# Query sums on VectorE, scaling on GpSimd ahead of the turn, and shared tokens' loads without overlap, in the opening of an attention and Fourier-mix kernel

## The chip, the cores and the metric

The kernel runs on one core of a Trainium2 chip. The metric is device time in microseconds (us), as a median of runs. In the profile PE is TensorE (matrix products; PEld its weight loads), DVE is VectorE, ACT is ScalarE, POOL is GpSimd, and SP is SyncE, which here issues most DMA loads. L12 is line 12 of the kernel. Each engine works through its own queue in order and waits for other engines by semaphores.

## The reference

```python
# q, k, v: (8, 8, 576, 64); w_ch1: (512, 2048); w_ch2: (2048, 512); all float32
def _attn_ref(q, k, v):
    q_s = np.exp(q - np.max(q, axis=-1, keepdims=True))
    q_s = q_s / (np.sum(q_s, axis=-1, keepdims=True) + 1e-09)
    k_s = np.exp(k - np.max(k, axis=2, keepdims=True))
    k_s = k_s / (np.sum(k_s, axis=2, keepdims=True) + 1e-09)
    kv = np.einsum('bhsd,bhse->bhde', k_s, v)
    return np.einsum('bhsd,bhde->bhse', q_s, kv).astype(np.float32)

def _moe_ref(x, w_ch1, w_ch2):          # x: attention output as (8, 576, 512)
    X = np.fft.fft(np.fft.fft(x, axis=1), axis=2)
    u = x + np.real(X).astype(np.float32)
    mu = np.mean(u, axis=-1, keepdims=True)
    var = np.mean((u - mu) ** 2, axis=-1, keepdims=True)
    un = (u - mu) / np.sqrt(var + 1e-06)
    return (u + np.maximum(un @ w_ch1, 0.0) @ w_ch2).astype(np.float32)
```

## The kernel before, in words

The eight sequences are worked on in turn. Each has 576 tokens: four tiles of 128 tokens (named by c and u, each 0 or 1), and 64 that are put together with those of a second sequence in a "shared" tile. Only the first 55 us differ between the two kernels: the opening, in which nothing of an earlier sequence is there to be overlapped with. After it TensorE does the two feed-forward products (L1169 and L1160 are the first of them, L1181 the second) of one sequence after another, and attention, Fourier mixing and norm of the next sequence run beside them.

The opening has its steps written out by hand: the string OPENING lists each step with a planned time, the steps are sorted by that time, and so every engine's queue gets its order. The planned time sets an order and nothing else. WARM adds groups of matrix products (L241) that have no use but to keep TensorE busy; they write the PSUM bank `ba`.

The steps, with the lines at which their instructions show:
- `k00` to `k03`: the first sequence's keys, two heads each. `max` (DVE L529), `exp` (ACT L532), `turn` (PE transposes L537), `four` (ACT copy of four transposed blocks, L540), `last` and `fifth` (transposes L545 and copy L548 of the last 64 tokens of all four), `kv` (PE L559). `k0 inverse` (DVE L551, L552) makes the reciprocal of the key sums, and `k0 scale0/1` (DVE L563) write the scaled product into `kvr`. `k10` to `k13` are the second sequence's keys.
- `A`, `B`, `C`, `D`: the first sequence's query tiles (c, u) = (0,0), (1,1), (0,1), (1,0); `t`: the shared tile. `max` (DVE L805), `less` (subtract the maximum: POOL L810, for `t` DVE), `exp` (ACT L814), `turn` (PE L822), `copy` (ACT L832, for `t` L842), `kv` (the product with `kvr`, PE L884, for `t` L914).
- The sums of the exponentials of A to D come from TensorE: `ones` (L876) multiplies the turned tile by a matrix of ones, `inverse` (DVE L890, L891) makes the reciprocals, and `out` (DVE L899) multiplies the product by them while it copies it from PSUM to the tile `x`. For `t` DVE does sum, reciprocal and multiplication ahead of the turn (L783 to L794).
- `t fold`, `t join` (DVE and POOL, L854 to L863) and `t parts`, `t folds` (ACT L921, L922; DVE L926 to L929) fold the shared tile for the Fourier transform. `tokens`, `columns`, `by`, `again` (DVE L945, L951, L958, L964 and L965) fold the four tiles; folds 0 and 2 read A and C, folds 1 and 3 read D and B.
- `b0` to `b4`: blocks of the first Fourier product (PE L997, L1000; copies on ACT L1007 to L1012). `m0`, `m1`: the second one for c = 0 and 1 (PE L1025; ACT L1034; DVE L1042; `add0` on DVE and `add1` on POOL, L1054 and L1055).
- `s00` and so on (statistics, DVE L1075), `root`, `scales`, `normal` (DVE L1096 for u = 0, ACT L1099 for u = 1), `turn` (PE L1105) and `laid` (DVE or ACT, L1114) end in the tile `unT`, which L1169 reads: first the columns of the tiles with c = 0, then those with c = 1.
- `c0`: the first of 32 "words" of the weights, which arrive as 64-bit values and are converted: `hi` and `lo` (ACT L375, L376), `shift` and `sign` (DVE L369, L372), `add` (POOL L377). Word i is needed by the i-th step of the first feed-forward product.

The loads are issued at the start (`loads_first`): keys, queries A/B, values, queries C/D, values, tables, the second sequence's keys and values and then the words on SP's queue, the shared tile's rows on ScalarE's.

Of the kernel before, what the change touches and what calls it, by code (L numbers as in the profile page):

```python
# [40 lines left out]
F32 = mybir.dt.float32  # L41
# [43 lines left out]
WARM = (3, 3), (24.7, 6), (41.9, 2), (43.45, 1), (44.5, 1)  # L85
OPENING = """
4.30 k00 max, 5.10 k00 exp, 5.50 k01 max, 6.05 k00 turn, 6.30 k01 exp, 6.65 k02 max, 7.06 k00 four,
7.25 k01 turn, 7.56 k02 exp, 7.75 k03 max, 8.32 k01 four, 8.51 k02 turn, 8.82 k03 exp, 8.90 A max, 9.50 B max,
9.58 k02 four, 9.65 A less, 9.77 k0 last, 10.10 k0 inverse, 10.27 k03 turn, 10.42 k0 fifth, 10.69 B less,
10.80 A exp, 11.20 k00 kv, 11.30 k03 four, 11.84 B exp, 11.85 A turn, 12.20 C max, 12.30 k01 kv, 12.45 A copy,  # L90
12.80 D max, 12.95 B turn, 12.95 C less, 13.40 A ones, 13.55 B copy, 13.99 D less, 14.10 C exp, 14.20 k02 kv,
14.35 A inverse, 14.85 C turn, 15.00 t max, 15.14 D exp, 15.30 k03 kv, 15.75 t less, 15.95 D turn,
16.35 k0 scale0, 16.40 B ones, 16.47 t exp, 16.80 k0 scale1, 17.14 t inverse, 17.25 B kv, 17.99 B inverse,
18.22 A kv, 18.35 C copy, 18.39 t normal, 19.01 B out, 19.19 t turn, 19.32 D copy, 19.63 k10 max, 19.69 C ones,
19.84 t copy, 20.30 A out, 20.43 k10 exp, 20.49 C kv, 20.92 C inverse, 21.39 t fold, 21.46 D ones,
22.09 t join, 22.26 D kv, 22.51 D inverse, 22.91 C out, 23.31 t kv, 23.53 D out, 24.15 tokens0, 24.21 k10 turn,
24.36 t parts, 24.77 tokens1, 25.39 columns0, 25.46 k10 four, 25.75 columns1, 26.23 by1, 26.59 by0,
26.80 c0 hi, 26.95 t folds, 27.45 c0 lo, 27.70 again0, 28.00 again1, 28.50 tokens3, 28.60 b0 times,
29.12 tokens2, 29.58 b1 times, 29.74 columns3, 29.80 b0 copies, 30.10 columns2, 30.56 b4 times, 30.58 by2,
30.78 b1 copies, 30.94 by3, 31.42 again2, 31.72 again3, 31.76 b4 copies, 32.22 k12 max, 32.32 b2 times,  # L100
32.89 c0 shift, 33.02 k12 exp, 33.30 b3 times, 33.59 c0 sign, 33.78 b2 copies, 34.19 k13 max, 34.28 k12 turn,
34.31 c0 add, 34.50 b3 copies, 34.86 k11 max, 35.05 k13 exp, 35.20 m0 times, 35.81 k12 four, 36.10 k13 turn,
36.31 m0 copy, 36.55 m1 times, 36.66 k11 exp, 36.81 m0 sums, 37.42 k13 four, 37.61 k1 last, 37.71 m0 add0,
37.92 m1 copy, 38.07 k11 turn, 38.27 k1 fifth, 38.39 m0 add1, 38.42 m1 sums, 38.77 k11 four, 38.92 k10 kv,
39.22 s00, 39.27 roots, 39.67 k11 kv, 39.69 m1 add1, 39.97 s01, 40.42 k12 kv, 40.87 root0, 40.99 m1 add0,
41.17 k13 kv, 41.67 scales0, 41.87 s11, 42.02 normal01, 42.62 s10, 42.77 turn01, 43.37 normal00, 43.52 root1,
43.87 scales1, 43.89 normal11, 43.95 laid01, 44.02 turn00, 44.22 normal10, 44.77 laid00, 44.87 turn10,
45.47 turn11, 45.62 laid10, 46.22 laid11, 53.00 k1 inverse, 53.30 k1 scale0, 53.60 k1 scale1"""
# [28 lines left out]
class _Block:  # L137
    def __init__(self, ctx, tc, q, kT, v, w1, w2, ft, cd, out):
# [38 lines left out]
        self.ones = c.tile([P, NR, H], F32, name="ones")  # L177
        nc.gpsimd.memset(self.ones[:], 0.0)
        for h in range(2):
            nc.gpsimd.memset(self.ones[64 * h:64 * h + 64].rearrange("p r h -> p (r h)")[:, h::H + 2], 1.0)  # L180

# [31 lines left out]
        self.unused = None  # L213
# [32 lines left out]
    def loads_first(self, fetch):  # L246
# [45 lines left out]
        def second(r):  # L292
# [7 lines left out]
                 lambda: values(0), lambda: queries(1), lambda: values(2), shared_firsts, self.tables,  # L300
# [214 lines left out]
    def first_keys(self, b):  # L515
# [4 lines left out]
        copy, box, top = nc.vector.tensor_copy if b == 0 else nc.scalar.copy, {}, {}  # L520
# [26 lines left out]
        def fifth():  # L547
            copy(self.fifth[64:], box["last"][64:])  # L548
# [26 lines left out]
    def opening(self, fetch, converted):  # L575
# [17 lines left out]
        named("t max,t less,t exp", self.q_exp_spread(shared, V))  # L593
        named("t inverse,t normal", self.q_inverse(shared, V, V))
# [203 lines left out]
    def q_exp_spread(self, it, e=None):  # L798
# [9 lines left out]
        def less():  # L808
            m = live[it].pop()[:].unsqueeze(2).to_broadcast([P, H, DH])
            (e or nc.gpsimd).tensor_tensor(out=heads(), in0=heads(), in1=m, op=ALU.add)  # L810
# [873 lines left out]
```

## Time and profile before

| | before |
|---|---|
| median of 3 runs | 1071.49 us (1070.27 to 1072.46) |
| the profiled execution | 1070.28 us |
| its span in the profile | 1068.5 us |
| PE busy / DVE busy / ACT busy / POOL busy | 1057.8 / 699.5 / 404.1 / 376.6 us |
| L1169, first half of the first feed-forward step, starts at | 49.08 us |
| L1160, its second step, starts at | 52.90 us |

A row of the timeline gives the start, the busy time, the engine, the line, the operation, the tiles (written <- read), how many instructions were merged into the row (x8), and in brackets how long the engine had been idle and what released it. One float32 product shows as two records.

### The profile page before, as it was taken

To read this page: it belongs to the slowest core of one execution; us is meant where nothing else is said; L and a number is where in the kernel's file an instruction comes from. 1 tells how busy PE (TensorE), PEld (TensorE's weight loads), DVE (VectorE), ACT (ScalarE), POOL (GpSimd) and SP (SyncE) were. 2 spreads that over 40 slices of the span, in tenths; PEclk is the share of its full clock that TensorE was granted. 3 is DMA by queue.
4 is the path that set the end of the run, shared out by engine and by line. 5 is a ranking of instruction groups with operands and counts; after the bars stand their busy time and mean duration, and the time that the engine had idled before them with its cause. 6 is when DMAs were issued, how large, how long until landed. Compare 5 with 4: busy or idle time off the path is not lost.

```text
span 1068.5 us, 16976 instructions
## 1 busy us (share of the span) xinstructions
PE 1057.8 (99%) x6394; PEld 922.1 (86%) x6394; DVE 699.5 (65%) x1350; ACT 404.1 (38%) x953; POOL 376.6 (35%) x317
## 2 busy tenths in 40 slices
PE   8999999999999999999999999999999999999998
PEld 7744556988898899889998999889988998899898
DVE  6897787685455884677555765678457754674563
ACT  5675534632245215531443234521552132231210
POOL 3262220265412733454515542374336450000000
PEclk9999999999999999999999999999999999999999
DMA  9496478648975576645755576557644575576464
GB/s 332 171 304 244 174 247 293 212 156 285 334 263 203 181 256 234 226 177 198 268 186 193 197 247 212 192 202 256 224 167 158 198 255 179 192 261 216 179 214 152
DMA packets 113546, 236.04 MB, mean 221 GB/s; under 512 B 23272, under 2 KB 74856, under 8 KB 102840
## 3 DMA queue, kind: packets, MB, share of 16 engines
q1 hardware_dynamic: 112904, 234.16, 63.9%
q8 instruction: 51, 0.84, 0.3%
q10 hardware_dynamic: 480, 0.52, 0.2%
q14 instruction: 31, 0.25, 0.1%
q0 software_dynamic: 80, 0.26, 0.1%
HBM read 199.79 MB, written 39.06 MB: 224 GB/s over the span
## 4 chain that ended last, share of the span: by engine, by line
PE 86%; DVE 3%; ACT 2%; issue 0%; ACTq 0%; DVEq 0%
PE bb L1244 15%; PE bb L1371 10%; PE bc L1244 10%; PE ba L1244 10%; PE bc L1371 7%; PE ba L1371 7%; PE bb L1341 5%; PE acc L716 3%; PE acc L884 2%; PE bc L1181 2%; PE bb L1460 2%; PE acc L997 2%; PE acc L1000 2%; PE acc L1025 2%; PE bc L1460 1%; PE ba L1460 1%
## 5 line engine op out<-in xcount | busy, mean ns | idle before, releaser
L1244 PE MATMUL bb<-unT,big 128*128 128x256 f32 x768 | 184.4, 380 | 0.8 <-DVE u L1214 0.8
L1244 PEld LDWEIGHTS bb<-unT,big 128*128 128x128 f32 x768 | 142.5, 190 | 20.3 <-DVE u L1214 2.3
L1256 ACT ACTIVATE big<-big 128x512 f32<-128x512 f32 x96 | 60.5, 630 | 195.0 <-DVE big L1255 194.5
L1244 PE MATMUL ba<-unT,big 128*128 128x256 f32 x512 | 123.8, 379 | 0.0
L1244 PE MATMUL bc<-unT,big 128*128 128x256 f32 x512 | 123.4, 379 | 0.0
L1214 DVE TENSOR_TENSOR u<-bb,s 128x512 f32<-128x512 f32 x66 | 45.6, 690 | 105.9 <-PE bb L1244 83.2
L383 POOL TENSOR_TENSOR big<-big 128x512 f32<-128x512 f32 x24 | 30.5, 1270 | 226.5 <-ACT big L1256 226.5
L1244 PEld LDWEIGHTS bc<-unT,big 128*128 128x128 f32 x512 | 94.7, 190 | 12.5 <-DVE big L1255 0.9
L1371 PE MATMUL bb<-big 128*128 128x128 f32 x848 | 105.1, 275 | 0.3 <-DVE u L1378 0.3
L1244 PEld LDWEIGHTS ba<-unT,big 128*128 128x128 f32 x512 | 94.4, 190 | 12.2 <-issue 0.5
L1371 PEld LDWEIGHTS bb<-big 128*128 128x128 f32 x848 | 99.6, 192 | 0.5 <-DVE u L1378 0.4
L1321 POOL TENSOR_TENSOR x<-x,big 128x512 f32<-128x512 f32 x45 | 57.7, 1297 | 62.7 <-issue 32.9
L1371 PE MATMUL ba<-big 128*128 128x128 f32 x640 | 79.6, 275 | 0.0
L766 ACT ACTIVATE q<-q,qm 128x64 f32<-128x64 f32 x248 | 67.2, 339 | 31.2 <-DVE qm L760 23.7
L1371 PEld LDWEIGHTS ba<-big 128*128 128x128 f32 x640 | 76.3, 192 | 1.2
L1317 DVE TENSOR_TENSOR big<-big 128x512 f32<-128x512 f32 x98 | 76.3, 818 | 0.0
L1341 PE MATMUL bb<-big 128*128 128x256 f32 x256 | 58.7, 381 | 0.0
L1378 DVE TENSOR_TENSOR u<-bb,s 128x256 f32<-128x256 f32 x40 | 16.9, 422 | 63.8 <-PE bb L1371 60.5
L1255 DVE TENSOR_TENSOR big<-bc,u 128x512 f32<-128x512 f32 x64 | 44.0, 687 | 21.8 <-PE bc L1244 21.0
L1120 POOL TENSOR_TENSOR unT<-unT 128x512 f32<-128x512 f32 x8 | 14.2, 1772 | 123.1 <-DVE unT L1120 100.8
L1341 PEld LDWEIGHTS bb<-big 128*128 128x128 f32 x256 | 48.2, 190 | 8.0 <-DVE big L1255 1.1
L1371 PE MATMUL bc<-big 128*128 128x128 f32 x416 | 51.5, 275 | 0.0
(265 smaller groups left out, 2025.1 us busy)
## 6 DMA issues: line engine op xcount, KB each, us to landing
big<-w2d SPq DMA_DIRECT2D x67, 1024.0 KB, 4.9
big<-w1s SPq DMA_DIRECT2D x64, 896.0 KB, 4.9
big<-w2s SPq DMA_DIRECT2D x16, 1024.0 KB, 6.4
big<-in_w_dram SPq DMA_DIRECT2D x21, 512.0 KB, 6.6
w2d<-big SPq DMA_DIRECT2D x42, 256.0 KB, 5.4
q<-in_q_dram SPq DMA_DIRECT2D x28, 256.0 KB, 6.5
k<-in_kT_dram SPq DMA_DIRECT2D x24, 288.0 KB, 5.8
v<-in_v_dram SPq DMA_DIRECT2D x24, 256.0 KB, 4.6
```

The source lines that it names most:

```text
L383: e1.tensor_tensor(out=to(4), in0=at(2), in1=at(3), op=ALU.add)
L716: nc.tensor.matmul(pk, lhsT=ks[:, c, :], rhs=v[:, c, :], start=(c == 0), stop=(c == NC - 1))
L766: nc.scalar.activation(q[:, h, :], q[:, h, :], ACT.Exp, bias=m[:, h:h + 1])
L1214: plus = lambda t: V.tensor_tensor(out=temp(t), in0=box["bb"][:], in1=box["s1"][:], op=ALU.add)
L1244: nc.tensor.matmul(bank()[:, i, :], lhsT=w[:, WA_AT[m], k * P:(k + 1) * P], rhs=self.unT[g][:, B_AT[m], k, :], start=first and i == 0 and ...
L1255: steps = [(0, lambda: V.tensor_tensor(out=hp(i), in0=bank()[:], in1=u()[:], op=ALU.add)), (0.8, lambda: nc.scalar.activation(hp(i), hp(i) ...
L1256: (0.8, lambda: nc.scalar.activation(hp(i), hp(i), ACT.Relu))]
L1317: e.tensor_tensor(out=to(o), in0=to(x), in1=to(y), op=op)
L1321: E.tensor_tensor(out=x, in0=x, in1=tile(m), op=ALU.add)
L1341: nc.tensor.matmul(box[name][:, i, :], lhsT=h[p][:, A_AT[m], i * P:(i + 1) * P], rhs=self.stream[n][:, p, :], start=p == 0 and (m != 1 or ...
L1371: nc.tensor.matmul(box[place[n]][:, i, :], lhsT=own(m)(A_AT[n])[:, f, :], rhs=w[:, r // 2, r % 2 * P:r % 2 * P + P], start=first and f == ...
L1460: nc.tensor.matmul(bank()[:, i, :], lhsT=h[p][:, A_AT[m], i * P:(i + 1) * P], rhs=w[:, p, :], start=first and i == 0 and p == 0, stop=p == ...
```

## The change

It makes the sums of A to D with reductions on DVE, from the exponentials ahead of the turn, and drops the product with ones, its matrix and the four separate inverses. All five sums go to one small tile; two inverse steps serve (t, C) and (D, A, B). For t, C and D POOL multiplies the exponentials by the reciprocals ahead of the turn. A and B are scaled when their products are copied out, as before. C's and D's products stay in PSUM (C's in bank `ba`, D's in `acc`), the folds read them there, and ScalarE copies them to `x` as well. `t less` goes from DVE to POOL, and `k0 fifth` from DVE to ScalarE. The turned queries are kept in four places of their own in the region of the converted weights instead of two rotating buffers. Word 1 is converted in the opening too. In the Fourier product and the norm c = 1 now goes ahead of c = 0. The shared tile's rows come by five loads on ScalarE's queue: one for the first rows of its four groups, four for the other 31 rows of each; before, four loads of 32 rows were partly overwritten by a fifth one on SP's queue. OPENING and WARM are written anew, and `first`, the time from which the later steps are counted, goes from 46.9 to 47.6.

```diff
-WARM = (3, 3), (24.7, 6), (41.9, 2), (43.45, 1), (44.5, 1)
+WARM = (3, 4), (23.6, 6), (42.1, 1), (43.9, 1)
 OPENING = """
...
+4.02 k00 max, 4.82 k00 exp, 5.16 k01 max, 5.82 k00 turn, 5.96 k01 exp, 6.24 k02 max, 6.96 k01 turn,
+7.04 k02 exp, 7.35 k03 max, 7.91 k00 four, 8.41 k01 four, 8.56 k02 turn, 8.75 A max, 8.91 k03 exp, 9.35 t max,
+9.50 A less, 9.78 k02 four, 9.91 k0 last, 9.95 k0 inverse, 10.30 B max, 10.43 k03 turn, 10.54 t less,
+10.61 k0 fifth, 11.13 k03 four, 11.26 k00 kv, 11.58 B less, 11.60 C max, 11.69 t exp, 12.19 A exp, 12.20 D max,
+12.61 k01 kv, 12.62 C less, 12.73 B exp, 12.84 A sum, 13.44 t sum, 13.66 D less, 13.73 B turn, 13.77 C exp,
+14.04 B sum, 14.18 k02 kv, 14.43 B copy, 14.64 C sum, 14.93 D exp, 15.30 A turn, 15.38 inverse1, 15.75 k03 kv,
+15.78 D sum, 15.88 t normal, 16.00 A copy, 16.52 inverse2, 16.93 C normal, 17.03 t turn, 17.10 k0 scale0,
+17.60 k0 scale1, 17.73 t copy, 17.98 D normal, 18.10 A kv, 19.00 C turn, 19.03 t fold, 19.45 D turn,
+19.70 C copy, 19.75 k10 max, 19.90 B kv, 20.20 D copy, 20.42 A out, 20.70 k10 exp, 20.75 t join, 20.88 D kv,
+21.05 B out, 21.78 C kv, 22.03 D out, 22.22 tokens1, 22.68 t kv, 22.93 C out, 22.93 tokens0, 23.55 columns1,
+23.58 k10 turn, 23.73 t parts, 23.91 columns0, 24.27 tokens2, 24.83 k10 four, 24.89 by0, 25.25 by1,
+25.61 t folds, 26.63 again0, 26.93 again1, 27.20 c0 hi, 27.68 tokens3, 27.83 b0 times, 27.85 c0 lo,
+28.30 columns2, 28.66 columns3, 28.80 c1 hi, 28.81 b4 times, 29.14 by3, 29.30 b0 copies, 29.50 by2,
+29.79 b1 times, 29.88 c1 lo, 29.98 again2, 30.28 again3, 30.43 b4 copies, 31.03 k11 max, 31.04 b1 copies,
+31.18 b2 times, 31.70 c0 shift, 31.83 k11 exp, 32.16 b3 times, 32.40 c0 sign, 32.70 b2 copies, 33.00 c1 shift,
+33.12 c0 add, 33.14 k11 turn, 33.41 b3 copies, 33.60 k12 max, 33.99 k11 four, 34.11 m1 times, 34.27 c1 sign,
+34.49 k12 exp, 34.87 k13 max, 34.99 c1 add, 35.21 m0 times, 35.46 m1 copy, 35.81 k13 exp, 35.96 m1 sums,
+36.31 k12 turn, 36.68 m0 copy, 36.81 k1 last, 36.91 m1 add0, 37.03 k12 four, 37.53 k1 fifth, 37.59 m1 add1,
+37.68 k13 turn, 37.71 s10, 38.03 roots, 38.18 k10 kv, 38.51 m0 sums, 39.33 k13 four, 39.46 m0 add0,
+39.53 k11 kv, 40.14 m0 add1, 40.14 s11, 40.88 k12 kv, 40.94 s00, 41.04 root1, 41.74 scales1, 41.94 s01,
+42.09 normal11, 42.23 k13 kv, 42.74 normal10, 42.84 root0, 43.24 scales0, 43.35 turn11, 43.59 normal00,
+43.59 normal01, 43.95 turn10, 44.10 laid11, 44.70 laid10, 44.88 turn00, 45.48 turn01, 45.63 laid00,
+46.23 laid01, 53.00 k1 inverse, 53.30 k1 scale0, 53.60 k1 scale1"""
...
-        self.ones = c.tile([P, NR, H], F32, name="ones")
-        nc.gpsimd.memset(self.ones[:], 0.0)
-        for h in range(2):
-            nc.gpsimd.memset(self.ones[64 * h:64 * h + 64].rearrange("p r h -> p (r h)")[:, h::H + 2], 1.0)
...
         def shared():
             flat = self.q[b:b + 2].rearrange("b s n -> (b s) n")
+            nc.scalar.dma_start(tail[0:P:Q], flat[::S // 2])
             for i in range(4):
                 a = i * S // 2 + P
-                nc.scalar.dma_start(tail[i * Q:(i + 1) * Q], flat[a:a + Q])
-
-        def shared_firsts():
-            load(tail[0:P:Q], self.q[b:b + 2].rearrange("b s n -> (b s) n")[::S // 2])
+                nc.scalar.dma_start(tail[i * Q + 1:(i + 1) * Q], flat[a + 1:a + Q])
...
-        named("t max,t less,t exp", self.q_exp_spread(shared, V))
-        named("t inverse,t normal", self.q_inverse(shared, V, V))
+        named("t max,t less,t exp", self.q_exp_spread(shared))
+        sums = self.small.tile([P, 5, H], F32, tag="sums", name="sums", bufs=1)
+        firsts = {"t": shared, **{n: own[n] for n in "CDAB"}}
+        heads = {n: self.live[it][0].rearrange("p (h d) -> p h d", h=H) for n, it in firsts.items()}
+        spread = {n: sums[:, i].unsqueeze(2).to_broadcast([P, H, DH]) for i, n in enumerate(firsts)}
+        for i, n in enumerate(firsts):
+            steps[f"{n} sum"] = lambda i=i, n=n: V.reduce_sum(sums[:, i], heads[n], axis=AX.X)
+            if n in "tCD":
+                steps[f"{n} normal"] = lambda n=n: G.tensor_tensor(out=heads[n], in0=heads[n], in1=spread[n], op=ALU.mult)
+            else:
+                self.live[own[n]].append(spread[n])
+
+        def inverse(s):
+            V.tensor_scalar(out=sums[:, s], in0=sums[:, s], scalar1=ATT_EPS, scalar2=None, op0=ALU.add)
+            V.reciprocal(sums[:, s], sums[:, s])
+
+        for i, s in enumerate((slice(0, 2), slice(2, 5))):
+            steps[f"inverse{i + 1}"] = lambda s=s: inverse(s)
...
-            named(f"{n} ones,{n} kv,{n} inverse,{n} out", self.q_times_kv(it))
+            named(f"{n} kv,{n} out", self.q_times_kv(it))
...
-        for i in range(1):
+        for i in range(2):
             some = converted(i)
...
-            qT = self.work.tile([P, NR, P], F32, tag="qT", name="qT", bufs=2)
-            self.nc.scalar.copy(qT[:], pt[:] if c == u else pt[:, :, ::-1])
+            if b == 0:
+                qT = self.w1sb[:, 1 + c + 2 * u, :].rearrange("p (r n) -> p r n", n=P)
+            else:
+                qT = self.work.tile([P, NR, P], F32, tag="qT", name="qT", bufs=2)[:]
+            self.nc.scalar.copy(qT, pt[:] if c == u else pt[:, :, ::-1])
...
-            px = self.acc((P, D))
-            box.insert(0, px)
+            if b == 0 and (c, u) != (1, 0):
+                n = {(0, 0): "bb", (1, 1): "bc", (0, 1): "ba"}[c, u]
+                t = self.ps.tile([P, 512], F32, tag=n, name=n)
+                px = t[:]
+            else:
+                px = self.acc((P, D))
+            box.append(px)
             box.extend(rec)
+            if b == 0 and c != u and not rec:
+                self.px[c, u] = px
...
-                e.tensor_tensor(out=eo[i][:, 0:D], in0=self.xpart(b, i % 2, 0), in1=self.xpart(b, i % 2, 1), op=op)
+                x, y = ((self.px.get((i % 2, u)) if b == 0 else None) for u in range(2))
+                x, y = (self.xpart(b, i % 2, u) if z is None else z for u, z in enumerate((x, y)))
+                e.tensor_tensor(out=eo[i][:, 0:D], in0=x, in1=y, op=op)
...
-    first, second, both = 46.9, 56, 77
+    first, second, both = 47.6, 56, 77
...
-    words = [first + 0.3, first + 1.4, *(first + 0.9 + 1.7 * i for i in range(1, NF - 2))]
+    words = [first + 0.7, *(first + 0.9 + 1.7 * i for i in range(1, NF - 2))]
```

More of the change, by code (lines that the diff above doesn't have):

```diff
@@ L84 @@
 DOWN = [(i, f) for n in range(4) for i in (2, 3, 0) for f in range(4 * n, 4 * n + 4)] + [(1, f) for f in range(NF)]
-WARM = (3, 3), (24.7, 6), (41.9, 2), (43.45, 1), (44.5, 1)
+WARM = (3, 4), (23.6, 6), (42.1, 1), (43.9, 1)
 OPENING = """
-4.30 k00 max, 5.10 k00 exp, 5.50 k01 max, 6.05 k00 turn, 6.30 k01 exp, 6.65 k02 max, 7.06 k00 four,
-7.25 k01 turn, 7.56 k02 exp, 7.75 k03 max, 8.32 k01 four, 8.51 k02 turn, 8.82 k03 exp, 8.90 A max, 9.50 B max,
-9.58 k02 four, 9.65 A less, 9.77 k0 last, 10.10 k0 inverse, 10.27 k03 turn, 10.42 k0 fifth, 10.69 B less,
@@ L90 @@
[L90 to L108, printed above, removed]
+4.02 k00 max, 4.82 k00 exp, 5.16 k01 max, 5.82 k00 turn, 5.96 k01 exp, 6.24 k02 max, 6.96 k01 turn,
@@ L212, in __init__ @@
         self.eo, self.unT, self.Z = {}, {}, {}
-        self.unused = None
+        self.unused, self.px = None, {}
         self.later = []
@@ L299, in loads_first @@
         order = [lambda: nc.gpsimd.memset(v[0:64, 4, :], 0.0), shared, table, *(lambda r=r: keys(r) for r in range(NR)), lambda: queries(0),
-                 lambda: values(0), lambda: queries(1), lambda: values(2), shared_firsts, self.tables,
+                 lambda: values(0), lambda: queries(1), lambda: values(2), self.tables,
                  *(lambda r=r: second(r) for r in range(NR)), *(lambda i=i: fetch(i) for i in range(11))]
@@ L519, in first_keys @@
         v = [v[:, :, r * P:(r + 1) * P] for r in range(NR)] if b == 0 else v
-        copy, box, top = nc.vector.tensor_copy if b == 0 else nc.scalar.copy, {}, {}
+        box, top = {}, {}
         rec = self.small.tile([P, NR], F32, tag="kinv", name="kinv", bufs=2)
@@ L547, in fifth @@
         def fifth():
-            copy(self.fifth[64:], box["last"][64:])
+            nc.scalar.copy(self.fifth[64:], box["last"][64:])
         def inverse():
@@ L796, in q_inverse, with q_exp_spread @@
         return [(0, inverse), (0, times)]
-    def q_exp_spread(self, it, e=None):
+    def q_exp_spread(self, it):
         nc, live = self.nc, self.live
@@ L809, in less @@
             m = live[it].pop()[:].unsqueeze(2).to_broadcast([P, H, DH])
-            (e or nc.gpsimd).tensor_tensor(out=heads(), in0=heads(), in1=m, op=ALU.add)
+            nc.gpsimd.tensor_tensor(out=heads(), in0=heads(), in1=m, op=ALU.add)
         def exp():
@@ L869, in q_times_kv @@
         box = []
-        def ones():
-            qT = self.live[it][0]
-            n = {(0, 0): "bb", (1, 1): "bc", (0, 1): "ba", (1, 0): "bb"}[c, u]
-            box.append(self.ps.tile([P, 512], F32, tag=n, name=n))
-            for r in range(NR):
-                nc.tensor.matmul(box[0][:, 0:H], lhsT=qT[:, r, :], rhs=self.ones[:, r, :], start=r == 0, stop=r == NR - 1)
         def times():
             qT, *rec = self.live.pop(it)
-            px = self.acc((P, D))
-            box.insert(0, px)
+            if b == 0 and (c, u) != (1, 0):
[5 more added lines that the diff above has]
+            box.append(px)
             box.extend(rec)
+            if b == 0 and c != u and not rec:
+                self.px[c, u] = px
             for r in range(NR):
@@ L885, in times @@
                                  stop=True)
-        def inverse():
-            t = self.small.tile([P, H], F32, tag="qrec", name="qrec", bufs=4)
-            sums = box.pop()
-            nc.vector.tensor_scalar(out=t[:], in0=sums[:, 0:H], scalar1=ATT_EPS, scalar2=None, op0=ALU.add)
-            nc.vector.reciprocal(t[:], t[:])
-            box.append(t[:].unsqueeze(2).to_broadcast([P, H, DH]))
         def out():
@@ L901, in out @@
             nc.scalar.copy(x, px)
-        return [(0, ones), (0, times), (1, inverse), (1.3, out)] if b == 0 else [(0, times), (1.3, out)]
+        return [(0, times), (1.3, out)]
     def t_times_kv(self, b):
@@ L1595 @@
         steps += at(t + 1.2 * i, some)
-    words = [first + 0.3, first + 1.4, *(first + 0.9 + 1.7 * i for i in range(1, NF - 2))]
+    words = [first + 0.7, *(first + 0.9 + 1.7 * i for i in range(1, NF - 2))]
     words += [first + dt for dt in (27, 31, 35, 39, 44, 49)] + [t + dt for dt in (-2, 2, 7.2, 10, 13, 26, 30, 33, 36, 39)]
-    for i, dt in enumerate(words, 1):
+    for i, dt in enumerate(words, 2):
         steps += at(dt, converted(i))
```

## The prediction

> **What bounds the kernel now.** I read the page's busy shares, then the list of PE's waits, then the timeline of each engine over the first 55 us (columns: start, busy time, engine, line, operation; idle time before it and its releaser in brackets).
>
> ```profile
> PE 1057.8 (99%) x6394; PEld 922.1 (86%) x6394; DVE 699.5 (65%) x1350; ACT 404.1 (38%) x953; POOL 376.6 (35%) x317
> ```
>
> ```profile
> PE ba L241 <- POOL kvr L155: 2.3, 1, 2.3
> PE acc L997 <- issue: 1.7, 1, 1.7
> ```
>
> PE hardly ever waits, and from L1160 on it does real work back to back. So the change, all of which lies ahead of that, is worth the shift of the start of L1160. The whole run shifts with it.
>
> ```profile
> 14.29 0.96 PE L876 MATMUL bb<-ones,qT 128*128 128x8 f32 x8
> 15.11 1.14 PE L559 MATMUL acc<-big,ks 128*128 128x128 f32 x8
> 25.21 1.06 PE L914 MATMUL acc<-kvr,F 128*128 128x128 f32 x8
> 30.98 0.73 PE L997 MATMUL acc<-ft,eo 128*128 128x144 f32 x4 [1.69 <-issue]
> 49.08 3.62 PE L1169 MATMUL ba<-unT,big 128*128 128x256 f32 x16
> 52.90 3.70 PE L1160 MATMUL bb<-unT,big 128*128 128x512 f32 x8 [0.20 <-POOL big L377]
> ...
> 15.29 0.17 DVE L890 TENSOR_SCALAR qrec<-bb 128x8 f32<-128x8 f32 x1 [1.83 <-PE bb L876]
> 18.06 0.86 DVE L563 TENSOR_TENSOR kvr<-acc,kinv 64x256 f32<-64x256 f32 x2 [0.98 <-PE acc L559]
> 24.74 1.36 DVE L899 TENSOR_TENSOR x<-acc,qrec 128x512 f32<-128x512 f32 x2
> 26.02 1.28 DVE L945 TENSOR_TENSOR eo<-x 128x512 f32<-128x512 f32 x2
> 40.26 0.86 DVE L1055 TENSOR_TENSOR x<-x,eo 128x255 f32<-128x255 f32 x1
> ```
>
> The reader sees a relay. PE works without a gap from 11 to 29 us and makes DVE idle twice (1.83 and 0.98). From 18.06 DVE is full, and PE waits for it (L997, 1.69 us: the folded columns, L965, end at 30.87). DVE then stays full up to the normalised tiles, apart from 1.02 us at 39 us.
>
> **One rule of this chip as the trace shows it.** Some DVE operations cannot start while a GpSimd operation runs.
>
> ```profile
> 10.23 0.70 DVE L551 TENSOR_SCALAR kinv<-kinv 128x4 f32<-128x4 f32 x1
> 9.86 2.04 POOL L810 TENSOR_TENSOR big<-big,qm 128x512 f32<-128x512 f32 x2 [4.55 <-DVE qm L805]
> L854 DVE COPY T<-F x4: 199/657/1205, 23.2 to 670.5; 128x16 f32<-128x16 f32 x4
> ```
>
> L551 works on four columns and takes 0.70: it ends with the first of the two POOL operations (about 10.90). L854 takes 0.20 when POOL is nearly done and 1.21 when a POOL operation has just begun. L1055 (0.42 when undisturbed) took 0.86 beside POOL's own addition. Reductions and operations with a PSUM input show no hold. The change puts four more operations of that kind on POOL's queue (t less and three normals), so I charge such holds.
>
> **The parts.**
>
> Off PE: four groups of L876, each 0.82 from start to start (14.29 to 15.11), 3.3 us out of the gapless stretch. Off DVE: four pairs L890/L891 (about 0.35, 1.4 together), t less 0.69, t normal 0.64, the fifth copy 0.69, C out and D out 0.64 each. Onto DVE: sums of A, B, C, D (reductions, 0.60 from start to start, 2.4), one more inverse pair (0.4), and word 1's shift and sign (1.3), which used to run at 50 us. DVE's total up to the normalised tiles falls only by about 0.5; what counts is that the sums lie at 13 to 17 us, where DVE had 2.8 us of idle time.
>
> Onto POOL: 1.04 each by L810. The skill's GPSIMD Engine Reference (section 8, Key points) puts VectorE at about twice GpSimd's speed for elementwise work; the rows here say 1.04 against 0.69. By the page the three normals would take 1.38 each and the end would be 1.0 later; the row is used.
>
> Hidden edits: the fifth load on ScalarE's queue adds 0.46 (a quarter of 1.84) to 0.62 (what L274 took on SP) ahead of the table load, so that load ends near 4.5, while the first exponential waits for a maximum that ends at 4.86. If that load has to wait for an earlier one to land, as SP's L290 did for 1.2 us, the exponential slips by some 0.3, under the longer warm-up, which (2.93 for 6 records, so 3.9 for 8) ends at 6.2 anyway. SP loses 0.62 ahead of the tables, keys and words; the DMA engines are full from 4 to 36 us, so landings stay. The dropped memsets cost nothing: POOL was idle from 5.3 to 9.9.
>
> Now the new order, carried forward with these rows (all estimates):
> - 9.03 to 11.9: A max, t max, the k0 inverse (held by A less to 10.93), B max. C max still waits for its queries (12.18), D max ends at 13.4. POOL subtracts A, t, B, C, D from 9.86 to 15.0. ScalarE, with the two k copies ahead of the last k exponential, reaches t exp at 12.1, A exp at 12.7, B exp at 13.2, C exp at 14.0.
> - Sums of A, t, B, C follow from 13.4 to 15.9, inverse1 to 16.3. POOL then runs t normal, C normal, D normal, 16.4 to 19.5. D sum, then inverse2: asked for at 16.9, held by t normal to 17.5, done at 17.7. Scales to 18.55 (the last k kv on PE ends near 17.0; it was 18.0).
> - t turn at 17.5, t copy at 18.5. The fold's first copy would start at 18.55 and is held by D normal to 19.5; the fold ends at 20.2 beside POOL's half. Then k10 max, A out, join, B out: 22.6. PE by then: A kv 18.6, C turn 19.5, D turn 19.9, B kv 20.4, D kv 21.3, C kv to 23.05.
> - tokens1 at 22.6, with D straight from PSUM; it was 26.02 for tokens0. One more fold (tokens2, 0.60) is now ahead of the first block: columns again end at 27.95 (30.87 before). The warm-up matmuls write the bank ba that holds C, so they wait for tokens2 (25.2) and end at 28.0: just not late. First block at 28.0 against 30.98, 3 us early.
> - Second half of the folds to 31.05, k11 max 31.7, both shifts and signs with the other maxima to 35.6 (word 1 costs 1.3 here). m1 sums to 36.55; m1 add0 1.21 beside POOL (as 39.91 to 41.12 before); s10, m0 sums, m0 add0 again beside POOL 1.2 (0.73 before, undisturbed), s11, s00, scales1, s01: 43.35. normal10, scales0, normal00: 44.75.
> - The last turn is 46.0 to 46.4, laid01 on ScalarE ends at 47.0. Here something is lost: L1169 takes the tiles of c = 0 first, and these now come last, so it cannot start behind the turns as it did at 49.08, but about 0.65 later. Start 47.05, end 50.67.
> - L1160 follows at once, as word 1 is long converted (the 0.20 in the row above goes): 50.67 against 52.90.
>
> Gain **2.2 us**. Profiled execution: 1070.28 (span 1068.5 and 1.8 around it), so 1068.1. It lay 1.2 under the median 1071.49, from which the forecast is counted: **1069.3**. A measurement of this kernel can tell about 0.2% (2.1 us) from no change, so this gain lies just beyond it.
>
> **The least certain term: PE's early speed.** Four transposes took 1.12 at 10.22 and 0.60 at 12.30: PE got fast only at about 11.3, after two gaps (0.58 and 0.35). The new order feeds PE without a gap from 2.31 to about 8.4, then with gaps of half a microsecond. Bounds: fast by 8.4 (no cost, used above since it is the longer gapless stretch), or slow up to 12.5, by which k0 last and the k03 turn each take 0.6 longer, ScalarE's exponentials come 0.9 later, and the gain is 1.3 to 1.6. TensorE: Matmul & The Clock Gate (Part 1) has the array at full speed after a busy window of some 3.4 us and back at half speed after an idle one; by it the new start would be fast earlier, and a thinly used stretch from 8.4 to 11.8 could undo it. No run here shows that.
>
> **Rivals.**
> 1. Given back (no measurable change). DVE's work fell by 0.5 only, so the engine that ends the opening has nearly the same sum. For: from 18.06 on it was full. Against: 2.8 us of idle time ahead of that are filled now. Each further hold by POOL costs up to 1.04 (at the fold, the two inverses), late PE speed 0.6 to 0.9. One or two of these leave 0.3 to 1.6: 1069.9 to 1071.2.
> 2. Slower: PE falls back to the slow rate once L876 is gone. PE's work from 11 to 25 us is about 11 us at the fast rate, with some 3 us of gaps now. At the slow rate (1.12 for 0.60, thus about double for transposes and the 128-wide products) the five groups A to D and t with their turns (0.90 and 0.44 each), 6.7 us, take 13. C kv then ends near 29 instead of 23, and L1160 starts 3 to 4 later than before: 1074.5 to 1075.5. It decides if the slow rate lasts beyond 16 us; against it speaks that the 1.69 gap at 29.3 did not slow the next group (0.73, then 0.65).
> 3. It does not start earlier because loads do not: C max waits for DMA, words 0 and 1 for theirs. Had word 1 landed after 29, ScalarE's c1 hi would hold up the copies of the first block. Words are issued from 19.30 on, and 512 KB at the 385 GB/s of that stretch is 1.4 us; word 0 had landed when it was converted at 28.00, so word 1 is there by 29.4 at the latest, more likely by 27; a miss costs 1: 1070.3. This belongs to case 1.
> 4. More gain: if the fold is not held (0.9) the start falls to 46.2: 1068.4.
>
> **Chances.** Forecast with 4: 0.48. Given back (1, 3): 0.43. Slower (2, or several unseen waits): 0.09. The forecast's own range is 1068.2 to 1069.9. For 8 in 10: below, case 4 and half a microsecond of spread between runs (1070.27 to 1072.46) give 1067.7; above, all of case 1 with that spread, 1072.2.
>
> **What would show it.** Right: no L876; L805 three times ahead of 12 us; the two L563 near 17.7; first L945 near 22.6; first L997 near 28.0; L1169 near 47.0 behind a short wait for ScalarE's L1114; no wait of L1160 for L377. Wrong: transposes still at 1.1 beyond 13 us; POOL's last of the three normals ending beyond 20.5; L1160 starting after 51.5; a wait of PE after that which the old run did not have.

## The result, and the profile after

The change made the kernel slower: 1082.27 us (median of 4 runs, 1081.77 to 1082.96) against 1070.88 (4 runs of the kernel before, 1069.91 to 1072.46). The ratio is 1.0105, 95% interval [1.0088, 1.0123]. The profiled execution took 1081.88, span 1080.1, so it is 11.6 longer than that of before (1068.5).

First the busy shares and PE's granted clock in 40 slices, from the page of the changed kernel:

```profile
PE 1056.6 (98%) x6360; PEld 920.3 (85%) x6360; DVE 697.9 (65%) x1343; ACT 404.9 (37%) x956; POOL 380.8 (35%) x318
PEclk8999999999999999999999999999999999999999
```

The work did shrink: 34 matmuls and 7 VectorE instructions less. PE's busy time is 1.2 lower and the span 11.6 longer, so PE waited. The granted clock falls short of that of before (9 in every slice) in the first slice alone, of 27 us, which points at the opening. PE's waits in the changed kernel (line, who released it; total, times, longest):

```profile
PE acc L553 <- DMA big<-in_v_dram: 5.4, 1, 5.4
PE tr L531 <- ACT big L526: 3.2, 1, 3.2
PE ba L237 <- POOL kvr L156: 2.3, 1, 2.3
PE ba L237 <- DVE eo L953: 1.4, 1, 1.4
```

L553 is k kv, here that of k00; L531 the first k turn; L237 the warm-up. The longest wait wasn't in the list of before; the second was, with 0.9 in all. It comes from ScalarE, which issues the shared tile's loads until 7.0 us (2.6 before) and only then loads its table, so that its first exponential starts at 8.42 (4.90 before). The timeline says when (VectorE's rows, then PE's; columns as in the prediction):

```profile
10.74 0.69 DVE L815 TENSOR_REDUCE qm<-big 128x8 f32<-128x512 f32 x1 [0.69 <-DMA big<-in_q_dram]
21.36 0.69 DVE L815 TENSOR_REDUCE qm<-big 128x8 f32<-128x512 f32 x1 [9.94 <-DMA big<-in_q_dram]
24.39 2.46 DVE L593 TENSOR_REDUCE sums<-big 128x8 f32<-128x512 f32 x4 [0.29 <-ACT big L824]
...
19.32 2.08 PE L553 MATMUL acc<-big,ks 128*128 128x128 f32 x8 [5.42 <-DMA big<-in_v_dram]
39.99 0.76 PE L1005 MATMUL acc<-ft,eo 128*128 128x144 f32 x4
59.02 3.69 PE L1177 MATMUL ba<-unT,big 128*128 128x256 f32 x16 [0.72 <-ACT unT L1122]
62.55 3.60 PE L1168 MATMUL bb<-unT,big 128*128 128x512 f32 x8
```

The first L815 is A max, the second t max, the maximum of the shared tokens. It waits 9.94 us for the loads on ScalarE's queue, and VectorE's whole queue stands behind it. The sums, forecast at 13.4, start at 24.39. PE waits at the same time for values (L553). L1168, the old L1160, starts at 62.55 instead of 52.90. That is 9.65 of the 11.6; the other 2 come later (below).

Why are those loads late? The DMA queues in the first 8 us of before and then of the changed kernel (packets, MB, share of 16 engines; q10 is ScalarE's queue):

```profile
q1 hardware_dynamic: 845, 1.69, 67.9%
q10 hardware_dynamic: 192, 0.26, 10.3%
```

```profile
DMA  0000000039936997999999989999679999620000
q1 hardware_dynamic: 832, 1.67, 63.2%
q10 hardware_dynamic: 27, 0.05, 2.0%
```

Before, all 128 rows (and their 64 completions) passed within 8 us. After, 27 packets did, and the first row shows the DMA engines nearly idle at the end of that window. This isn't contention: something passes one row at a time. The single packets in the trace say what. Before, each of the four loads ends in 16 packets of 4 bytes, the completions. After, each of the four loads of 31 rows ends in one, and 2048-byte rows follow each other every 0.12 us (median) until 20.7 us. **A load of 31 rows went through one DMA engine.**

The Trainium skill states this ("DMA: Bandwidth & Descriptors", section "Why a DMA increments its semaphore by 16 and not by 1", at "How many engines (k)"): a DMA runs on the largest number of engines, 16 at most, that divides the slowest dimension of its source and of its destination. By it 32 rows get 16 engines, and 31, a prime, one. The completions agree.

SP's loads suffer too. The SP queue's own longest waits in the changed kernel:

```profile
SPq L279 <- DMA big<-in_q_dram: 6.2, 1, 6.2
SPq L318 <- DMA big<-in_q_dram: 3.4, 1, 3.4
SPq L280 <- DMA big<-in_q_dram: 2.5, 1, 2.5
```

SP may not issue the values (L279) until a slow load has landed, so the values that L553 needs land at 19.3. The trace's semaphores show the reason: the first loads of all queues take eight of them in turn, and a later load waits for the one that had its semaphore before. L279 takes over that of the first load of 31 rows.

### The profile page after: what moved, and what is told of

The parts are those of the page before. It is cut to its first block, busy times and chain, and to the rows that moved or that the text cites. A ratio compares the mean times of both kernels' runs of the same rounds, so it can differ in the third digit from the quotient of the medians.

```text
span 1080.1 us, 16917 instructions
## 1 busy us (share of the span) xinstructions
PE 1056.6 (98%) x6360; PEld 920.3 (85%) x6360; DVE 697.9 (65%) x1343; ACT 404.9 (37%) x956; POOL 380.8 (35%) x318
## 4 chain that ended last, share of the span: by engine, by line
PE 83%; DVE 3%; ACT 2%; DMA 1%; issue 0%; ACTq 0%; DVEq 0%
PE bb L1252 15%; PE bb L1379 10%; PE bc L1252 10%; PE ba L1252 10%; PE bc L1379 6%; PE ba L1379 6%; PE bb L1349 5%; PE acc L726 2%; PE acc L897 2%; PE bb L1468 2%; PE acc L1005 2%; PE acc L1008 2%; PE bc L1189 2%; PE acc L1033 1%; PE bc L1468 1%; PE ba L1468 1%
```

## The experiments

The table gives each kernel's last row landed on ScalarE's queue, the completions on that queue in the first 25 us, and the start of L1168 (or its counterpart), all from the profiled execution. The ratio is to the kernel before in the same session, where its median was 1070.54 to 1071.47, so kernels compare by their ratios. Executions of one kernel differ by 1 to 4.5 us: a row of a profile shows a mechanism, and only the ratio shows what a small gain is worth.

| kernel | last row | completions | L1168 | median us | ratio [95%] |
|---|---|---|---|---|---|
| before | 6.5 | 64 | 52.90 | | 1 |
| changed | 20.7 | 8 | 62.55 | 1082.27 | 1.0105 [1.0088, 1.0123] |
| e1_rows32_spare | 8.1 | 68 | 52.34 | 1072.66 | 1.0009 [0.9999, 1.0019] |
| e2_before_rows31 | 19.9 | 8 | 60.89 | 1078.54 | 1.0064 [1.0047, 1.0081] |
| e3_rows30 | 10.5 | 68 | 54.49 | 1073.02 | 1.0013 [1.0003, 1.0022] |
| e9_rows29 | 17.2 | 16 | 59.79 | 1079.60 | 1.0085 [1.0068, 1.0102] |
| e10_rows27 | 11.6 | 56 | 56.15 | 1075.22 | 1.0042 [1.0028, 1.0056] |
| e4_loads_as_before | 7.0 | 64 | 56.06 | 1076.66 | 1.0050 [1.0033, 1.0067] |
| e5_eight_loads | 6.9 | 64 | 52.17 | 1071.51 | 1.0004 [0.9994, 1.0013] |
| e6_outs_behind | | | 52.46 | 1071.76 | 1.0005 [0.9996, 1.0015] |
| e7_word3_early | | | 51.82 | 1070.68 | 0.9995 [0.9985, 1.0005] |
| e8_mended | 6.5 | 64 | 51.23 | 1070.19 | 0.9987 [0.9978, 0.9996] |
| e11_word1_back | | | 51.32 | 1072.20 | 1.0010 [1.0001, 1.0019] |
| e12_mended_word1_back | | | 50.66 | 1070.67 | 1.0001 [0.9991, 1.0010] |

### Is it the 31 rows?

**Four loads of 32 rows, in the changed kernel.** The fifth load stays but goes to an unused place, so that four rows of the shared tokens hold other queries:

```diff
-            nc.scalar.dma_start(tail[0:P:Q], flat[::S // 2])
+            nc.scalar.dma_start(self.big[0:P:Q, 5 * D:6 * D], flat[::S // 2])
...
-                nc.scalar.dma_start(tail[i * Q + 1:(i + 1) * Q], flat[a + 1:a + Q])
+                nc.scalar.dma_start(tail[i * Q:(i + 1) * Q], flat[a:a + Q])
```

> The changed kernel, with four loads of 32 rows again and the load of the four first rows aimed at an unused place in the region of the weights; the four first rows of the shared tile are therefore not the right ones. Nine loads still come first, the order of all steps is the changed one. Theory rows (a load of 31 rows is served by one DMA engine, a load of 32 by sixteen): the shared tile is there by 8 us, t max runs before 11 us, L1169 starts near 47 to 48, time 1068 to 1071. Theory count (nine loads for eight semaphores hold the queues up): as the change, 1080 or more. Theory schedule (sums on VectorE and scaling by GpSimd are slow in themselves): 1080 or more.

```profile
9.66 1.28 DVE L815 TENSOR_REDUCE qm<-big 128x8 f32<-128x512 f32 x2 [0.90 <-DMA big<-in_q_dram]
14.19 2.45 DVE L593 TENSOR_REDUCE sums<-big 128x8 f32<-128x512 f32 x4
24.09 0.69 DVE L953 TENSOR_TENSOR eo<-acc,x 128x512 f32<-128x512 f32 x1 [0.67 <-ACT x L907]
...
29.78 0.76 PE L1005 MATMUL acc<-ft,eo 128*128 128x144 f32 x4
48.81 3.69 PE L1177 MATMUL ba<-unT,big 128*128 128x256 f32 x16 [0.72 <-ACT unT L1122]
52.34 3.60 PE L1168 MATMUL bb<-unT,big 128*128 128x512 f32 x8
```

A max and t max now follow each other without a wait. The sums start 10.20 earlier than in the changed kernel and L1168 10.21: the loads of 31 rows account for the opening's whole loss. The number of loads (still five) isn't the cause. L1177 (48.81, where 47 to 48 was expected) and the time (1072.66 for 1068 to 1071) came later than expected; what is left is followed up below.

**The changed loads alone, in the kernel before**; the order and the sums are as before:

```diff
+            nc.scalar.dma_start(tail[0:P:Q], flat[::S // 2])
...
-                nc.scalar.dma_start(tail[i * Q:(i + 1) * Q], flat[a:a + Q])
-
-        def shared_firsts():
-            load(tail[0:P:Q], self.q[b:b + 2].rearrange("b s n -> (b s) n")[::S // 2])
+                nc.scalar.dma_start(tail[i * Q + 1:(i + 1) * Q], flat[a + 1:a + Q])
...
-                 lambda: values(0), lambda: queries(1), lambda: values(2), shared_firsts, self.tables,
+                 lambda: values(0), lambda: queries(1), lambda: values(2), self.tables,
```

> The kernel before with the change's loads alone (first rows and four loads of 31 rows on ScalarE's queue, nothing on SP's). Theory rows: first exponential near 8.4 us, values and with them k00 kv near 19 us, time 1078 to 1082. Theory count: the same. Theory schedule: no change, 1070 to 1072.

```profile
17.24 2.08 PE L557 MATMUL acc<-big,ks 128*128 128x128 f32 x8 [3.82 <-DMA big<-in_v_dram]
20.48 1.28 DVE L803 TENSOR_REDUCE qm<-big 128x8 f32<-128x512 f32 x2 [7.01 <-DMA big<-in_q_dram]
```

1078.54: the loads alone cost 7 us. The price is paid by other hands: t max stands late in this order, and it is the values (3.82) and the second queries (7.01), held back behind the slow loads, that come late. In the change's order, which takes the shared tokens second, it is t max that pays, with its 9.94.

**30, 29 and 27 rows.** The rows left out at the end of each group come with one, two and four more loads of four rows each, as here for 30:

```diff
-                nc.scalar.dma_start(tail[i * Q + 1:(i + 1) * Q], flat[a + 1:a + Q])
+                nc.scalar.dma_start(tail[i * Q + 1:(i + 1) * Q - 1], flat[a + 1:a + Q - 1])
+            nc.scalar.dma_start(tail[Q - 1:P:Q], flat[P + Q - 1::S // 2])
```

> The changed kernel with each load of 31 rows cut to 30, and the four last rows by one more strided load: six loads on ScalarE's queue, ten in all. Theory rows (30 rows go over fifteen DMA engines, four rows over four): the shared tile is there by 9 us, ScalarE's first exponential up to 1 us later than in the kernel before, time 1069 to 1072. Theory count: slower than the change, 1082 or more. Theory schedule: 1080 or more.

> Each of the four loads brings 29 rows; the two rows that are missing at the end of each group come with two more loads of four rows. Main theory (a load is spread over the largest number of engines, at most sixteen, that divides its rows): 29 has no such divisor but 1, so 116 rows still pass through one engine one after the other. At the 15.65 us that the change took for 124 rows they take 14.6: the t maximum starts near 20.4 instead of 21.36, only some 30 packets of ScalarE's queue land in the first 8 us, L1168 starts near 61.5, and the time is 1080 to 1082. Rival (31 rows are bad only because the load ends one row short of a group of 32): 29 rows are as good or as bad as 30, so about 180 packets in the first 8 us, L1168 near 54.5, 1072 to 1074.

> Each of the four loads brings 27 rows; the other four of each group come with four more loads of four rows, so that ScalarE's queue has nine. Main theory: 27 is divided by 9, so nine engines serve a load. The rows land within the first 8 us (over 130 packets of this queue in the window), L1168 starts at 54 to 56, since more loads wait for earlier ones to land, and the time is 1072.5 to 1075. Rival (an odd number of rows is what hurts, or any number that is not two short of 32 or more): as with 31, t maximum near 20, L1168 near 61, 1079 to 1082.

ScalarE's queue in the first 8 us, for 30, 29 and 27 rows in this order:

```profile
q10 hardware_dynamic: 182, 0.25, 9.8%
```

```profile
q10 hardware_dynamic: 37, 0.07, 2.3%
```

```profile
q10 hardware_dynamic: 152, 0.23, 11.0%
```

The completions count the engines: with 30 rows 68 = 4 x 15 + 2 x 4; with 29, 16 = 4 x 1 + 3 x 4; with 27, 56 = 4 x 9 + 5 x 4. So 15, 1 and 9 engines, the largest divisors up to 16. An odd number is not what hurts (27), nor a start off a multiple of 32 (30 and 27 start there too), nor that a load is one row short of 32 (29 is three short). Some sizes were missed: with 30 rows the time was 1.0 above the 1069 to 1072 expected; with 29 rows t max started at 18.06, not 20.4, as rows passed faster (0.082 us apart), and the time was 0.4 below what was expected. With 27, L1170 was just later and the time just above (1075.22 for 1072.5 to 1075). There ScalarE pays for issuing:

```profile
6.67 2.28 ACTq L270 DMA_DIRECT2D big<-in_q_dram  x4
8.97 1.28 ACT L274 ACT_TABLE_LOAD   x1 [8.97 <-DMA big<-in_q_dram]
```

The loads past the fifth wait for earlier ones to land, and the table load and the first exponential (10.38) stand behind them in ScalarE's order.

**All loads as before, in the changed kernel** (first rows again on SP's queue, behind the second values):

```diff
-            nc.scalar.dma_start(tail[0:P:Q], flat[::S // 2])
...
-                nc.scalar.dma_start(tail[i * Q + 1:(i + 1) * Q], flat[a + 1:a + Q])
+                nc.scalar.dma_start(tail[i * Q:(i + 1) * Q], flat[a:a + Q])
+
+        def shared_firsts():
+            load(tail[0:P:Q], self.q[b:b + 2].rearrange("b s n -> (b s) n")[::S // 2])
...
-                 lambda: values(0), lambda: queries(1), lambda: values(2), self.tables,
+                 lambda: values(0), lambda: queries(1), lambda: values(2), shared_firsts, self.tables,
```

> The changed kernel with the loads of the kernel before: four of 32 rows on ScalarE's queue, the first rows on SP's queue behind the values. Theory rows: no load is slow, but the first rows land behind the values near 14 us, and t max, which now stands ahead of B max, holds VectorE until then: some 3 us lost against the forecast of 1069.3, so 1071 to 1074. Theory count: eight loads first, so the same. Theory schedule: 1080 or more.

```profile
14.88 0.69 DVE L817 TENSOR_REDUCE qm<-big 128x8 f32<-128x512 f32 x1 [4.78 <-DMA big<-in_q_dram]
18.45 0.66 PE L834 MATMUL tr<-ident,big 128*128 128x128 f32 x4 [3.51 <-ACT big L826]
```

Here t max waits 4.78 for the four first rows, and PE 3.51. The order does need the first rows earlier than SP brought them, so moving them was right; cutting row 0 off the four loads was not. The result was higher than the 1071 to 1074 expected: L1170 started 3.16 later than L1160 before, and more was lost after it.

**No fifth load at all** (e1 without it):

```diff
-            nc.scalar.dma_start(self.big[0:P:Q, 5 * D:6 * D], flat[::S // 2])
```

> e1 without the load of the four first rows, which are left out: eight loads come first in place of nine. Theory count (the ninth load waits for an earlier one to land and with it stands ScalarE's table load, and the queries come later): first exponential at 4.9 in place of 5.77, A max at 9.03 in place of 9.66, L1168 at 51.5 to 51.7 in place of 52.34, time 0.5 to 0.9 below e1. Rival (the start of the opening is hidden behind the sums and POOL): L1168 within 0.2 of e1.

A max came at 9.39, not 9.03, and L1167 at 52.17: 0.17 earlier than in e1, where 0.6 to 0.8 was expected. The fifth load is a part at most of what makes the start late: without it A max starts 0.27 earlier.

### What is left after the mend, and where does it go?

With its loads mended (e1) the opening starts L1168 0.56 early, 1.67 later than forecast, and even those 0.56 are gone at the end. Five more kernels asked for both.

**C and D out behind the tokens** (e1, with the two places exchanged in the written order).

```diff
-21.05 B out, 21.78 C kv, 22.03 D out, 22.22 tokens1, 22.68 t kv, 22.93 C out, 22.93 tokens0, 23.55 columns1,
+21.05 B out, 21.78 C kv, 22.22 tokens1, 22.24 D out, 22.68 t kv, 22.93 tokens0, 22.95 C out, 23.55 columns1,
```

> e1 with D out and C out on ScalarE right behind tokens1 and tokens0 instead of ahead of them. Theory reads in order (two engines' reads of one PSUM tile are kept in the order of the program, so the fold waited for ScalarE's copy): tokens1 starts near 23.4, at once behind D kv and B out, in place of 24.09, first block 0.7 to 0.9 earlier, L1168 near 51.5, time 0.5 to 0.9 below e1. Rival (the fold waited for the product, and the copy only ended with it): no change.

```profile
24.18 0.69 DVE L953 TENSOR_TENSOR eo<-acc,x 128x512 f32<-128x512 f32 x1
25.03 0.69 DVE L953 TENSOR_TENSOR eo<-x,ba 128x512 f32<-128x512 f32 x1 [0.15 <-PE ba L897]
```

The wait of tokens1 for ScalarE (0.67 on L907 in e1) is gone: two engines read the same PSUM tile in the order in which the code has them, and D out's copy stood ahead. From A max to the first block it took 19.79 instead of 20.12, a gain of 0.33; 0.7 to 0.9 was expected. A max itself came late in this run (10.11), and the time shows no clear gain over e1 (ratio 1.0005 for 1.0009).

**Word 3's conversion one place earlier** (e1, ahead of the first relu on ScalarE). The reason is VectorE's timeline in e1:

```profile
53.70 0.69 DVE L363 TENSOR_SCALAR big<-acc 128x512 int32<-128x512 int32 x1 [3.00 <-ACT acc L369]
55.63 1.04 DVE L545 TENSOR_SCALAR kinv<-kinv 128x4 f32<-128x4 f32 x1
```

Word 2 was converted 2 us earlier than before, but word 3 waits 3.00 for ScalarE, and the k1 inverse (0.22 before) is held by POOL to 1.04. From 58 to 73 us VectorE ran 0.5 to 0.8 later than before and near 83 us still 0.25 (83.58 for 83.33), though PE was 0.66 earlier, and at 110 us PE waited for that chain:

```profile
110.47 1.16 PE L897 MATMUL acc<-kvr,qT 128*128 128x128 f32 x8 [0.40 <-ACT qT L845]
```

```diff
-    words = [first + 0.7, *(first + 0.9 + 1.7 * i for i in range(1, NF - 2))]
+    words = [first + 0.7, first + 1.6, *(first + 0.9 + 1.7 * i for i in range(2, NF - 2))]
```

> e1 with the conversion of word 3 ahead of the first relu in ScalarE's queue. Theory words (behind the opening VectorE's chain of conversions is the second bound, it starts again only behind the first relu, VectorE is idle for 3.00 us there, and so an earlier L1168 is lost again by 190 us): the 3.00 us idle go, the query turns near 100 us and the norm near 167 us come about 1 us earlier against L1168, the waits of PE at 110 and 167 us go, time 0.5 to 1.0 below e1. Rival (the lost 1 us is chance or comes from elsewhere): no change.

The idle 3.00 became 2.23, the hold went (0.24), VectorE's row near 83 us came at 82.83, and PE's wait at 110 us fell to 0.16. PE's wait at 167 us (0.46) was still there, and near 162 us it waited 0.72.

Seven profiles (the changed kernel, e1, e6, e7, e8, e11, e12) agree that VectorE's chain sets the loss at 110 us. Take how far VectorE lags behind PE at its row near 83 us, against before: 0.91 in e1 (0.25 late, with PE 0.66 early). Less 0.56, this is what PE has lost by 112 us (0.35 in e1), in all seven within 0.02; where it is under 0.56, as in e8, PE loses nothing.

**Word 1 back behind the opening** (in e1; the c1 steps also leave the written order):

```diff
-        for i in range(2):
+        for i in range(1):
             some = converted(i)
...
-    words = [first + 0.7, *(first + 0.9 + 1.7 * i for i in range(1, NF - 2))]
+    words = [first + 0.3, first + 1.4, *(first + 0.9 + 1.7 * i for i in range(1, NF - 2))]
-    for i, dt in enumerate(words, 2):
+    for i, dt in enumerate(words, 1):
```

> The mended loads (32 rows each, first rows once more to an unused place), and word 1's conversion back behind the opening, in the places of the kernel before; all else as changed. What is asked is why the gain at L1168 of the mended kernel (0.56 us early) is gone at the end. Theory A (VectorE's conversions are a second bound from 50 us on: in the mended kernel word 3's stands behind the first relu on ScalarE and VectorE idles 3.00 us, then runs 0.5 us later than before from 57.5 on, and PE waits 0.40 for it near 110 us): word 1 fills that idle time, so VectorE's row near 53.7 idles about 1.2 us as before, PE's wait near 110 us is under 0.1, and the opening, lighter by 1.3 us of VectorE, starts L1168 near 51.1. The wait for the store near 151 us (2.45 before, 3.08 mended) stays at 3 to 4, so that the end lies 0.5 to 1.3 us before that of the kernel before: ratio 0.9987 to 0.9997. Rival (the later start is simply a bound of the transfers, whatever the order of the words): L1168 near 51.1 too, but PE's waits near 110 and 165 us grow to 2 us or more together, and the ratio stays at 1.000 to 1.001.

L1146 started at 51.32, 1.02 earlier than in e1, and it was all given back: PE waited 1.10 at 110 us. The rival is right. The idle time was half filled (1.69), but the hold stayed (1.04), and then VectorE waited for a store to land, which it didn't in e1:

```profile
74.08 0.42 DVE L399 TENSOR_TENSOR s<-u,big 128x256 f32<-128x256 f32 x1 [1.15 <-DMA w1s<-s]
```

So its row near 83 us came at 83.66, no earlier than e1's 83.58: the transfer set the time here, not the conversions. By the ratios (1.0010 for 1.0009) it makes no difference to e1 where word 1 is converted.

**The mended kernel**: four loads of 32 rows on ScalarE's queue, the first rows on SP's between the first values and the second queries, t behind B in the maxima, subtractions, exponentials and sums, the outs behind the tokens, word 3 early:

```diff
...
+        def shared_firsts():
+            load(tail[0:P:Q], self.q[b:b + 2].rearrange("b s n -> (b s) n")[::S // 2])
...
-                 lambda: values(0), lambda: queries(1), lambda: values(2), self.tables,
+                 lambda: values(0), shared_firsts, lambda: queries(1), lambda: values(2), self.tables,
```

> The changed kernel with eight evenly spread loads first (four of 32 rows on ScalarE's queue, the first rows on SP's between the first values and the second queries), t behind B in maxima, subtractions, exponentials and sums, the copies of C and D behind the folds, word 3 early. All computed. If the theories rows, count, reads and words hold together: L1168 at 50.7 to 51.3, time 1068.3 to 1069.8, faster than the kernel before by 0.15 to 0.3 per cent. If only rows holds: 1071 to 1073.

```profile
22.95 0.69 DVE L955 TENSOR_TENSOR eo<-acc,x 128x512 f32<-128x512 f32 x1
28.66 0.76 PE L1007 MATMUL acc<-ft,eo 128*128 128x144 f32 x4
47.70 3.69 PE L1179 MATMUL ba<-unT,big 128*128 128x256 f32 x16 [0.72 <-ACT unT L1124]
51.23 3.60 PE L1170 MATMUL bb<-unT,big 128*128 128x512 f32 x8
```

1070.19 (1068.05 to 1071.23, 11 runs), ratio 0.9987 [0.9978, 0.9996]: the only kernel here whose interval lies below 1, faster than the kernel before by 0.13%. That is less than the 0.15 to 0.3 expected, though L1170 came as expected. It shows no wait at 110 us. L1170 starts 1.67 early and the span is 0.9 shorter. **With word 1 back** this kernel starts L1148 at 50.66 but ends no earlier (span 1067.8):

> The kernel that mends four things (four loads of 32 rows, first rows on SP's queue between the values and the second queries, t behind B, outs behind the tokens), now with all words of the conversion in the places of the kernel before. Theory A: the opening is lighter by 1.3 us of VectorE, L1170 starts at 49.9 to 50.5 instead of 51.23, no wait near 110 us, the store's wait near 150 us at 3 to 4: 1068.3 to 1069.8, ratio 0.9975 to 0.999. Rival: L1170 as early, but all of it given back by waits near 110 and 165 us: 1070 to 1071, ratio 0.999 to 1.

1070.67, ratio 1.0001 [0.9991, 1.0010], with 0.81 of PE's time lost at 110 us: the rival again.

The second loss comes from a wait near 151 us that is in every kernel, before's own included. VectorE rewrites a buffer that a store still reads. Before, the changed kernel, and the mended one:

```profile
151.09 0.43 DVE L427 TENSOR_TENSOR spare<-big 128x256 f32<-128x256 f32 x1 [2.45 <-DMA w2s<-spare]
```

```profile
162.77 0.43 DVE L421 TENSOR_TENSOR spare<-big 128x256 f32<-128x256 f32 x1 [3.91 <-DMA w2s<-spare]
```

```profile
150.19 0.43 DVE L423 TENSOR_TENSOR spare<-big 128x256 f32<-128x256 f32 x1 [3.37 <-DMA w2s<-spare]
```

In the mended kernel the wait is 0.92 longer than before, and PE loses 0.90 against before near 161 and 166 us. In the changed kernel it is 1.46 longer, and PE loses 1.44; in all thirteen kernels the two agree within 0.03 us. From the issue of that store to this row pass 6.37 us before, 6.30 in the kernel before with the changed loads, and 6.9 to 7.9 in all kernels with the changed opening. Why the store lands later there was not tried and stays open.

## Why the prediction was wrong

The forecast was 1069.3, range 1067.7 to 1072.2; measured were 1082.27, 13 us above the forecast, 10 above the range, and slower where faster was the likeliest.

- **The step that failed: "Hidden edits".** It charged the fifth load with 0.46 to 0.62 of issuing and left the rest as it was: "the DMA engines are full from 4 to 36 us, so landings stay". The loads were costed by number and bytes. The four of 31 rows looked like the four of 32, but ran on one engine each; t max, placed at about 9.6, came at 21.36, and the first exponential, whose slip was put at some 0.3, came 3.5 late (8.42 for 4.90). e1, e2, e3, e9 and e10 show it, and at L1168 it costs 10.21 (e1 against the changed kernel).
- **"The whole run shifts with it": half right.** PE does work back to back from L1160 on, but VectorE's chain of conversions, with its waits for stores, stands behind it as a second bound. Against the kernel before, PE in the changed kernel is 9.55 behind after L1168, 10.25 after the wait at 110 us, and 11.68 after the waits near 162 and 167 (in the times of the kernel before). In e1, 0.66 ahead became 0.5 behind. By e1 this would have cost the forecast gain about a microsecond, even with the right loads.
- **The opening, read from e1.** L1168 forecast at 50.67 came at 52.34, 1.67 late. The start was late by 0.63 (A max 9.66 for 9.03), the sums by 0.79, tokens1 by 1.49, the first block by 1.78. Thus some 0.8 at the start and 0.7 at "tokens1 ... with D straight from PSUM", where ScalarE's copy of the same tile came first (0.67). The tail was right: first block to L1177 took 19.03 for 19.05 forecast, with 0.72 of waiting for laid for about 0.65.
- **The holds by POOL were right.** In e1 the second inverse took 0.64, the fold's first copy 0.68 (forecast 0.9), and L1063 0.86 both times.
- **"PE's early speed".** In e1 the transposes at 9.22 took 0.66 (1.11 at 8.43 before): PE was fast by then, the bound I took. That the longer warm-up did it is likely, but no run changes it alone. In the changed kernel PE fell back. The windows of the changed kernel, 10 to 20 and 20 to 25 us (busy us of PE, PEld, DVE, ACT, POOL with counts; granted clock; DMA share; GB/s):

```profile
10.00:20.00 10.00, 4.38 (x19) 3.52 (x20) 0.74 (x2) 4.22 (x10) 1.04 (x1) 0.67 0.71 217
20.00:25.00 5.00, 3.94 (x20) 3.73 (x20) 3.31 (x8) 1.67 (x3) 2.87 (x3) 0.63 0.67 216
```

L553 took 2.08 at 19.32 and 1.06 at 25.42. This is the slow rate of rival 2, as a consequence of waiting and not as the cause: the clock fell while PE waited for loads (it was 1.00 in both windows before). In e2, L557 took the same 2.08 behind its wait of 3.82 with a granted clock of 1.00 in the window, so that number doesn't show every slow stretch. The page "TensorE: Matmul & The Clock Gate" (Part 1) has the array back at half speed after an idle window, and the rows of the changed kernel agree with it.

- **Rivals.** Rival 3 doubted the words' loads, not those that were changed; the loads' shape had no rival at all. Rival 1 (given back) is what e1 shows, though for another reason than the one given.
- **Small slips in the working.** By its own terms the range's lower end is 1067.9 (1068.4 less 0.5), not 1067.7, and a slow group of transposes costs 0.5 more by its rows (1.12 for 0.60), not 0.6. Neither bears on the result.

## What to carry to other kernels

Before a load is cut, count the divisors of its rows: one row fewer took these loads from sixteen DMA engines to one. In the profile such a load shows as few packets of its queue in a window, one completion per load and DMA engines that idle. A gain in the opening counts only as far as the next engine's chain moves along with it; compare each engine's timeline behind the change, not only that of the one that is always busy.

## What the runs showed of the hardware

- On a single engine, rows of 2048 bytes came mostly 0.08 to 0.17 us apart (changed kernel); the last of 124 landed at 20.7 us.
- A load's issue can wait for the landing of an earlier one whose semaphore it takes over, on its own queue or another: in the changed kernel SP's L279 waited 6.2 us for one on ScalarE's, and with 27 rows ScalarE's L270 waited from 4.1 to 6.67 us for one of its own.
- A VectorE operation on four columns (L545, the k1 inverse) took 1.04 where a POOL addition had just begun (e1, e11) and 0.22 to 0.24 where one was about to end (before, e7): each time it ended with that addition.
